# A decode kernel's result in two halves instead of four quarters, one store on each queue, and the last wait as an instruction of its own

## The chip, the cores and the metric

The kernel runs on one core of one Trainium2 chip. The metric is the device time of one execution in microseconds (us); a run is one execution. The profile's "span" is shorter: it goes from the first to the last of the program's own instructions. All timed runs quoted are of the state "fast", or "unknown" where a kernel was looked at once.

Names: PE is TensorE (matmuls), PEld its weight loads, DVE is VectorE, ACT is ScalarE, POOL is GpSimd, SP is SyncE (it issues the loads). A q after a name is that engine's instruction sequencer, and L687 is line 687 of the kernel.

## The reference, cut to what matters

One token for each of 4 batch entries attends over a cache of 8192 positions (16 query heads on 8 KV heads of 256). The output projection's result `s` is multiplied by a gate `g`, which comes from a small MLP, and added to the input.

```python
B, Sq, D = 4, 1, 448
Hq, Hkv, Sk, Dh = 16, 8, 8192, 256
...
x = A_x
xn = _layernorm(x, axis=-1)
s = _A_ref(xn, A_k_cache, A_v_cache, A_wq, A_wo)     # attention, then @ wo (4096 x 448)
g = _silu(_B_ref(xn, B_w1, B_w2, B_w3, B_w4))
return x + s * g                                     # 4 x 1 x 448, bf16
```

The two caches are 268 MB. The result is 4 rows of 448 numbers.

## The kernel before

SyncE streams K, V and the weights in. Of `wo`, the last heads' pieces ("LATE") are loaded last of all. The result is made in four quarters of D: quarter `i` lies on 4 of the 32 partitions that begin at `32 * i`, so that its matmuls run in their own 32 columns of TensorE, beside those of the three others (in the trace, the first four of the projection start at 651.411, 651.415, 651.418 and 651.421 us and are 0.21 to 0.22 us long each).

```python
NQD = 4
DQ, PQ = D // NQD, P // NQD                  # 112 columns, 32 partitions
...
def store(eng, i):
    eng.dma_start(out2d[:, i * DQ:(i + 1) * DQ], out_b[i * PQ:i * PQ + Bn, :]
                  ).then_inc(S["dout"], 16)
...
# SyncE, after its last load                 # ScalarE, after its last exp
sp.wait_ge(S["v_out"], 1)                    act.wait_ge(S["v_out"], 1)
store(sp, 0)                                 store(act, 2)
store(sp, 1)                                 store(act, 3)
sp.wait_ge(S["dout"], 16 * NQD)
...
def take(eng, name, n=1):                    # a wait with an update: an instruction of its own
    eng.wait_ge(S[name], n).then_inc(S[name], -n)
...
def f_o(hs, stop=False):                     # TensorE, the projection (L687)
    for hq in hs:
        for dh in range(NHALF):
            for i in range(NQD):
                ins = pe.matmul(o_ps[i * PQ:(i + 1) * PQ, 0:DQ],
                                OT[:, hq // REP, hq % REP, dh, :],
                                wo_sb[:, hq, dh, i * DQ:(i + 1) * DQ], ...)
...
take(pe, "dwl0", 16)                         # TensorE, the very end
f_o(LATE[0])
take(pe, "v_ot")
f_o(range(HQ - REP, HQ))
for i in range(1, len(LATE)):
    take(pe, "dwl%d" % i, 16)
    ins = f_o(LATE[i], i == len(LATE) - 1)
ins.then_inc(S["p_o"], 1)
...
v.wait_ge(S["p_o"], 1)                       # VectorE (L526, L528)
c(v.tensor_tensor(res[:, :], o_ps[:, 0:DQ], sg4[:, :], ALU.mult))
c.sync()
v.tensor_tensor(out_b[:, :], res[:, :], x4[:, :], ALU.add).then_inc(S["v_out"], 1)
```

A plain `wait_ge` with nothing after it but the end of the program is put on the next instruction of that engine; for SyncE that is the branch to the barrier at the program's end (in the raw records below it starts 0.017 us after the last landing of a store).

## Time and profile before

| | value |
|---|---|
| device time, median of the first 3 runs | 658.67 us (658.19 to 659.90) |
| span of the profiled run | 656.0 us |
| device time minus span of that run | 2.18 us |
| last piece of `wo` landed (semaphore records) | 652.378 us |
| from there to the end of the span | 3.620 us |

The view of stretches gives, for each stretch of time, its length, each engine's busy time (with the number of instructions), the granted TensorE clock as a share of full speed, the share of the DMA engines that is busy, and the rate. For the kernel before:

```profile
core 0: us, PE busy (x) PEld busy (x) DVE busy (x) ACT busy (x) POOL busy (x), PEclk, DMA share, GB/s
31.00:620.00 589.00, 510.73 (x9331) 445.18 (x9328) 246.01 (x496) 239.21 (x341) 9.40 (x58) 0.89 1.00 431
620.00:652.40 32.40, 29.26 (x499) 22.81 (x499) 11.11 (x25) 8.35 (x15) 0.20 (x1) 0.94 0.94 397
652.40:656.00 3.60, 0.38 (x8) 0.17 (x8) 0.55 (x2) 0.00 (x0) 0.00 (x0) 0.50 0.01 1
```

For 589 us the share of the DMA engines that is busy is 1.00: the kernel is bound by its loads. Only the last line, 3.6 us in which nothing is loaded, belongs to the change. The timeline of that tail (start, length, engine, line, what; in brackets the idle time before it and who ended it), kernel before, weight loads left out:

```profile
start us, us, engine line op out<-in xcount [idle before <-releaser]
651.41 0.93 PE L687 MATMUL pst<-wo_sb,OT 128*32 128x112 bf16 x40 [0.45 <-PEq L244]
...
652.51 0.38 PE L687 MATMUL pst<-wo_sb,OT 128*32 128x112 bf16 x8 [0.17 <-PEq L244]
652.94 0.27 DVE L526 TENSOR_TENSOR res<-pst,sg 128x112 f32<-128x112 f32 x1 [1.65 <-PE pst L687]
653.25 0.27 DVE L528 TENSOR_TENSOR out_b<-res,x 128x112 bf16<-128x112 f32 x1
653.55 0.66 SPq L184 DMA_DIRECT2D out_dram<-out_b  x2
653.55 0.62 ACTq L184 DMA_DIRECT2D out_dram<-out_b  x2
```

TensorE has done 40 of its last 48 matmuls when the last `wo` lands at 652.378; it waits, and does the last eight. Then two VectorE operations in series, then two stores on each queue.

The timeline leaves out waits, branches and drains. SyncE's last instructions, from the raw records of the same trace (start in us, kind, length in ns); the last landing of a store is at 655.252:

```
653.548 DMA_DIRECT2D 347
653.936 DMA_DIRECT2D 274
655.269 COMPARE_BRANCH 33      <- the branch that carries the wait for the stores
655.713 DRAIN 77               <- 0.444 us later
655.935 EVENT_SEMAPHORE 17     <- the barrier
```

### The profile page before, as it was taken

What the parts mean: (1) busy time and instruction counts of PE and PEld (TensorE: products, weight loads), DVE (VectorE), ACT (ScalarE), POOL (GpSimd) and SP (SyncE); (2) the same over time, 40 slices, a digit from 0 to 9 for tenths busy, and PEclk for the clock granted to TensorE, in tenths of its full rate; (3) what the DMA queues carried; (4) which work ended last, traced back from release to release, by engine and by line L of the source; (5) the groups of instructions that cost most, each with busy time, mean ns of one, the idle gap of its engine ahead of it and who ended that gap; (6) DMA issues with size and microseconds to landing.
All of it is one profiled execution on the core that took longest, in us unless ns stands there. A gap on an engine that the chain in (4) does not pass through costs nothing. (4 is left out here: it accounts for less than half of the span.)

```text
span 656.0 us, 22934 instructions
## 1 busy us (share of the span) xinstructions
PE 554.9 (85%) x9969; PEld 475.1 (72%) x9969; DVE 276.4 (42%) x593; ACT 256.2 (39%) x364; POOL 13.4 (2%) x77
## 2 busy tenths in 40 slices
PE   1899997988888988888897888898888898888897
PEld 0487886876766887677787766787677688766774
DVE  7453554443443443344443443444344443343441
ACT  4144544442433443334443333444333344433340
POOL 2000000000000000000000000000000000000000
PEclk9698999887899888789987888988778987888998
DMA  8999999999999999999999999999999999999996
GB/s 361 442 412 424 439 424 440 424 440 424 440 424 440 424 440 426 438 426 440 424 435 430 434 430 434 430 434 432 432 432 432 432 432 432 434 430 434 432 423 279
DMA packets 12369, 279.13 MB, mean 426 GB/s; under 512 B 1220, under 2 KB 3272, under 8 KB 3784
## 3 DMA queue, kind: packets, MB, share of 16 engines
q1 hardware_dynamic: 12336, 278.99, 99.3%
q8 instruction: 7, 0.11, 0.1%
q14 instruction: 2, 0.02, 0.0%
q10 hardware_dynamic: 24, 0.01, 0.0%
HBM read 278.99 MB, written 0.00 MB: 425 GB/s over the span
## 5 line engine op out<-in xcount | busy, mean ns | idle before, releaser
L588 PE MATMUL pst<-ident_b,kn 128*128 128x128 bf16 x4096 | 347.2, 239 | 79.0 <-PEq L244 76.4
L294 ACT ACTIVATE kT<-pst 128x1024 bf16<-128x1024 bf16 x224 | 229.5, 1025 | 360.7 <-ACTq L244 359.9
L588 PEld LDWEIGHTS pst<-ident_b,kn 128*128 128x128 bf16 x4096 | 275.4, 108 | 84.9 <-issue 84.3
L292 DVE COPY kT<-pst 128x1024 bf16<-128x1024 bf16 x288 | 197.5, 692 | 264.6 <-DVEq L244 264.6
L600 PE MATMUL psc<-qc,kT 128*128 128x2 bf16 x4096 | 178.4, 164 | 0.0
L600 PEld LDWEIGHTS psc<-qc,kT 128*128 128x128 bf16 x4096 | 157.4, 98 | 28.5 <-issue 28.1
L639 PE MATMUL psv<-vb,pT 128*4 128x512 bf16 x1056 | 86.3, 378 | 0.0
L618 PE MATMUL psm<-sel,po 128*128 128x2 f32 x272 | 36.8, 257 | 0.5 <-PEq L244 0.5
L618 PEld LDWEIGHTS psm<-sel,po 128*128 128x128 f32 x272 | 34.7, 196 | 0.9 <-issue 0.9
L639 PEld LDWEIGHTS psv<-vb,pT 128*4 128x4 bf16 x1056 | 22.2, 82 | 15.0 <-issue 0.5
L452 DVE TENSOR_REDUCE rmax<-psc 128x2 f32<-128x128 f32 x32 | 9.3, 292 | 48.5 <-DVEq L244 48.5
L470 DVE COPY po<-psv 128x512 f32<-128x512 f32 x34 | 23.5, 692 | 3.0 <-DVEq L244 2.3
L457 DVE TENSOR_REDUCE gmax<-psm 2x1 f32<-2x128 f32 x32 | 8.9, 279 | 34.7 <-DVEq L244 34.7
L316 ACT ACTIVATE pT<-psc,negb 128x64 bf16<-128x64 f32 x66 | 20.6, 333 | 5.4 <-ACTq L244 5.4
L612 PEld LDWEIGHTS psm<-diag,ones_f 2*128 2x128 f32 x66 | 14.1, 264 | 6.5 <-issue 5.7
L279 POOL COPY qc<-qT 128x4 bf16<-128x4 bf16 x32 | 5.9, 186 | 585.7 <-DVEq L469 568.4
L612 PE MATMUL psm<-diag,ones_f 2*128 2x2 f32 x66 | 16.8, 322 | 1.1 <-PEq L244 0.9
L316 ACT ACTIVATION_READ_ACCUMULATOR pT<-psc,negb 128x1 f32 x66 | 13.6, 206 | 0.0
L608 PEld LDWEIGHTS psm<-ident_f,rmax 128*2 128x2 f32 x32 | 2.6, 80 | 14.0 <-issue 14.0
L536 PE MATMUL pst<-ident_b,xn_b 4*128 4x4 bf16 x14 | 0.6, 161 | 13.6 <-DVE xn_b L365 8.9
L630 PE MATMUL psm<-rowsum,ones_f 128*128 128x2 f32 x64 | 11.6, 251 | 0.0
L536 PEld LDWEIGHTS pst<-ident_b,xn_b 4*128 4x128 bf16 x14 | 0.5, 99 | 13.6 <-issue 8.9
(101 smaller groups left out, 119.8 us busy)
## 6 DMA issues: line engine op xcount, KB each, us to landing
kn<-in_A_k_cache_dram SPq DMA_DIRECT2D x32, 4096.0 KB, 25.7
vb<-in_A_v_cache_dram SPq DMA_DIRECT2D x31, 4096.0 KB, 31.3
vb<-in_A_wq_dram SPq DMA_DIRECT2D x1, 3584.0 KB, 11.5
vb<-in_B_w_dram SPq DMA_DIRECT2D x2, 1568.0 KB, 16.4
wo_sb<-in_A_wo_dram SPq DMA_DIRECT2D x1, 2688.0 KB, 44.0
kn<-in_A_v_cache_dram SPq DMA_DIRECT2D x1, 2048.0 KB, 25.1
kn<-in_A_v_cache_dram SPq DMA_DIRECT2D x1, 1024.0 KB, 27.1
kn<-in_A_v_cache_dram SPq DMA_DIRECT2D x2, 512.0 KB, 28.3
```

The lines of the kernel that those rows point to most:

```text
L292: engine.tensor_copy(dst, src).then_inc(S["v_ev"], 1)
L294: engine.activation(dst, src, ACT.Copy).then_inc(S["a_ev"], 1)
L316: ins = act.activation(pv_p[:, :, hh], sc[:, :, hh], ACT.Exp, bias=negb[:, s, hh:hh + 1], scale=SCALE, accum_out=rowsum[:, s, hh:hh + 1])
L452: v.tensor_reduce(rmax[:, :], psc[h % 2][:, 0:NCH * REP].rearrange("p (k h) -> p h k", h=REP), AX.X, ALU.max).then_inc(S["v_rmax"], 1)
L457: v.tensor_reduce(gmax[:, :], psm[0:REP, 0:P], AX.X, ALU.max).then_inc(S["v_s"], 1)
L470: v.tensor_copy(po[:, slot], psv[:, 0:CP * DH]).then_inc(S["v_po"], 1)
L588: ins = pe.transpose(dst[:, t * P:(t + 1) * P], kn[:, h % 2, GC * j + kl, half * P:(half + 1) * P], ident_b[:, :])
L600: ins = pe.matmul(psc[h % 2][:, kk * REP:(kk + 1) * REP], kT[:, j % RING, t * P:(t + 1) * P], qc[:, h % 2, half, :], start=(half == 0), st ...
L612: pe.matmul(psm[:, P:P + REP], ones_f[0:REP, :], diag[:, :], start=True, stop=True).then_inc(S["p_m2"], 1)
L618: ins = pe.matmul(dst(dh)[:, 0:width], po[:, slot, i * DH + dh:(i + 1) * DH:NHALF], sel[:, i, 0:width], start=(i == 0), stop=(i == CP - 1))
L630: pe.matmul(psm[:, P + REP:P + 2 * REP], ones_f[:, :], rowsum[:, h % 2, :], start=True, stop=True)
L639: ins = pe.matmul(psv[o:o + CP * REP, 0:CP * DH], pT[:, h % 2, kk * REP:(kk + CP) * REP], src[:, kk:kk + CP, :].rearrange("p c d -> p (c d)"),
```

## The change

The intent: one store on each queue instead of two, which needs each store to cover half of D, hence halves instead of quarters; and no wait on the final branch. Cut to its core:

```diff
-    DQ, PQ = D // NQD, P // NQD
+    NDG = 2
+    DQ, PQ = D // NDG, P // NQD             # now 224 columns; still 32 partitions a group
+    DP = NDG * PQ                           # 64
...
-        res = sb("res", [P, DQ], F32)       # the same for x4, xn4, sg4, bout, out_b
+        res = sb("res", [DP, DQ], F32)
...
             store(sp, 0)
-            store(sp, 1)
-            sp.wait_ge(S["dout"], 16 * NQD)
+            take(sp, "dout", 16 * NDG)
...
-            store(act, 2)
-            store(act, 3)
+            store(act, 1)
...
-                for i in range(NQD):        # VectorE's prologue copies into x4 and xn4,
+                for i in range(NDG):        # TensorE's f_o and its two f32 products with selb
...
-            c(v.tensor_tensor(res[:, :], o_ps[:, 0:DQ], sg4[:, :], ALU.mult))
+            c(v.tensor_tensor(res[:, :], o_ps[0:DP, 0:DQ], sg4[:, :], ALU.mult))
```

More of the change, by code (lines that the diff above doesn't have):

```diff
@@ L61, in bass_recurrent_scan__gqa_block_cached__mixer_s_mlp__decode_kernel @@
     NQD = 4
-    DQ, PQ = D // NQD, P // NQD
-    assert D == NQD * DQ
+    NDG = 2
+    DQ, PQ = D // NDG, P // NQD
+    DP = NDG * PQ
+    assert D == NDG * DQ
     NCH = SK // P
@@ L138, in bass_recurrent_scan__gqa_block_cached__mixer_s_mlp__decode_kernel @@
         xn2_f = sb("xn2_f", [Bn, D], F32)
-        x4 = sb("x4", [P, DQ], F32)
-        xn4 = sb("xn4", [P, DQ], F32)
-        sg4 = sb("sg4", [P, DQ], F32)
-        res = sb("res", [P, DQ], F32)
+        x4 = sb("x4", [DP, DQ], F32)
+        xn4 = sb("xn4", [DP, DQ], F32)
+        sg4 = sb("sg4", [DP, DQ], F32)
+        res = sb("res", [DP, DQ], F32)
         xn2_b = sb("xn2_b", [Bn, DK, P // 2, 2], BF16)
         junk = sb("junk", [Bn, D], F32)
-        bout = sb("bout", [P, DQ], F32)
-        out_b = sb("out_b", [P, DQ], BF16)
+        bout = sb("bout", [DP, DQ], F32)
+        out_b = sb("out_b", [DP, DQ], BF16)
         st = sb("st", [Bn, 16], F32)
@@ L174, in bass_recurrent_scan__gqa_block_cached__mixer_s_mlp__decode_kernel @@
         h2_ps = psv
-        hs_ps = psm[:, 2 * P:2 * P + DQ]
+        hs_ps = psm[0:DP, 2 * P:2 * P + DQ]
         o_ps = pst[0]
@@ L573, in prog_pe @@
             take(pe, "v_h2")
-            for i in range(NQD):
+            for i in range(NDG):
                 ins = pe.matmul(hs_ps[i * PQ:(i + 1) * PQ, :], selb[:, :],
@@ L685, in f_o @@
                     for dh in range(NHALF):
-                        for i in range(NQD):
+                        for i in range(NDG):
                             ins = pe.matmul(o_ps[i * PQ:(i + 1) * PQ, 0:DQ],
@@ L732, in finish @@
                 take(pe, "v_a")
-                for i in range(NQD):
+                for i in range(NDG):
                     pe.matmul(o_ps[i * PQ:(i + 1) * PQ, 0:DQ], selb[:, :],
```

## The prediction

The four terms came to -0.36 - 0.36 + 0.22 + 0.6 = +0.1 us, from 658.67 to 658.8 us. No term is cut from it, only reasons, where the cuts are marked: in point 1 a general statement of how stores report landings (the trace of the kernel before shows four landings for each store, 16 in all), in point 4 a rule of when the clock falls and how that shifts between executions, which no trace had shown. The trace had shown half clock from 651.70 us on; the +0.6 within its range is the author's estimate. The figures for 224 columns are estimates from that trace, where matmuls of 112 columns in one group start 0.049 us apart at full clock and 0.093 at half, and those of the gate's f32 product 0.19 at half clock; doubled, that is about what the points say. That the wider rows cost nothing visible, and that only the branch costs the 0.44 us, were assumptions. In point 3 the trace has 216 ns at 56 columns and not 222, which makes it 1.05 ns a column, and still about +0.12.

> **What bounds it now.** Loads. The table of stretches shows the DMA share at 1.00 and 431 GB/s from 31 to 620 us, while TensorE waits for tiles in every pass. The semaphore landings put the last piece of wo at 652.38 us of a 656.00 us span. The change touches no load. It can move only the last 3.6 us (and a little of the prologue).
>
> **The tail now, read from the trace records (us).** Last wo lands 652.38; last eight matmuls (32 rows x 112) 652.51 to 652.89, their semaphore 652.915; VectorE multiply 652.94, 0.274 long; add 653.25, 0.274 long; the two queues issue their first stores at 653.55, their second at 653.85 (ScalarE) and 653.94 (SyncE). Landings come in four groups of four, 0.18 apart: 654.64-654.71, 654.82-654.89, 655.00-655.07, 655.18-655.25. SyncE's wait sits on a branch (655.269); its next instruction starts only at 655.713, 0.44 later. End barrier to 656.00.
>
> **What the change does, on that chain.**
>
> 1. Stores, -0.36: one store per queue leaves only the first two groups, so the last landing comes about 1.345 after the issue instead of 1.704. [...] Rows of 448 B instead of 224 B should cost nothing visible.
> 2. Wait, -0.36: as an instruction of its own it needs no branch. On GpSimd a semaphore instruction before the block's end is followed by the drain after 0.08 (632.252 to 632.333), where SyncE's branch took 0.44.
> 3. VectorE, +0.22: both result operations go from 112 to 224 columns on half the partitions. Tensor-tensor took 222 ns at 56 columns and 275 ns at 112, so about 0.95 ns a column: about +0.11 each, estimated.
> 4. TensorE, +0.1 to +0.95, estimate +0.6: four column groups become two, with twice the columns. 48 matmuls become 24, but each group still gets 12, of 224 columns. Starts in one group are 0.049 apart at full clock at 112; so about 0.096 at 224, and 0.187 at half clock. The clock records show half clock from 651.70. Starting at 651.41, the twelve then end near 653.6 instead of 652.9: no longer hidden behind the last load, but bound by TensorE itself. [...] this trace's half-clock stretches are multiples of 3.41. [...] if the clock is full, only +0.1 remains; if half throughout, +0.95.
> 5. Off the path: the f32 matmul of the gate becomes about 0.37 longer at half clock near 24.6, delaying the first transposes at 30.8. SyncE issues the third K load at 42.5 while the queue is busy until the wo landing at 47.3, so absorbed. Half as many prologue copies on VectorE: also absorbed. The f32 matmul at 648.3 ends before the piece that lands at 648.85 is taken.
>
> **Sum.** -0.36 -0.36 +0.22 +0.6 = +0.1 us. From 658.67: 658.8 us, range 657.6 to 660.0, mostly the scatter of runs (658.19 to 659.9 before). Faster by over 2%: 1%; within 2%: 98%; slower: 1%.
>
> **What will show it.** 8 landings instead of 16 on the result's semaphore, last about 1.35 after the issue; SyncE's drain about 0.1 after its wait; VectorE operations of about 0.385; last matmul's semaphore 0.1 to 0.95 later after the last wo landing than 0.537; DMA share and last wo landing unchanged.
>
> **What would make it wrong.** Full clock in the tail in most runs (then about -0.4); landings of 448 B rows slower; a branch that stays; a load that starts later because of the prologue.

## The result, and the profile after

| | before | after |
|---|---|---|
| median device time | 658.58 us (658.19 to 660.07, 6 runs) | 658.34 us (657.41 to 659.91, 6 runs) |
| ratio after to before | | 0.9991, 95% interval 0.9974 to 1.0007 |
| device time minus span | 2.18 us (the profiled run) | 1.67 us (mean of 6 runs, 1.61 to 1.81) |

A ratio here is the mean time of one kernel's fast runs over that of the other's fast runs of the same rounds, so it is not quite the ratio of the medians. The two kernels are the same within the noise.

The same two views, kernel after:

```profile
core 0: us, PE busy (x) PEld busy (x) DVE busy (x) ACT busy (x) POOL busy (x), PEclk, DMA share, GB/s
31.00:620.00 589.00, 511.11 (x9332) 445.64 (x9331) 245.94 (x496) 238.91 (x341) 9.40 (x58) 0.89 1.00 431
620.00:652.40 32.40, 29.12 (x465) 22.70 (x467) 11.21 (x25) 8.34 (x15) 0.20 (x1) 0.94 0.94 397
652.40:656.00 3.60, 1.62 (x18) 1.15 (x14) 0.77 (x2) 0.00 (x0) 0.00 (x0) 0.50 0.01 1
```

```profile
start us, us, engine line op out<-in xcount [idle before <-releaser]
...
651.61 2.41 PE L687 MATMUL pst<-wo_sb,OT 128*32 128x224 bf16 x24 [0.50 <-PEq L245]
654.06 0.38 DVE L526 TENSOR_TENSOR res<-pst,sg 64x224 f32<-64x224 f32 x1 [2.61 <-PE pst L687]
654.47 0.38 DVE L528 TENSOR_TENSOR out_b<-res,x 64x224 bf16<-64x224 f32 x1
654.88 0.35 SPq L186 DMA_DIRECT2D out_dram<-out_b  x1
654.89 0.28 ACTq L186 DMA_DIRECT2D out_dram<-out_b  x1
```

The loads are untouched: 1.00 and 431 GB/s as before. In the tail, the 24 matmuls are one block of 2.41 us without a gap. TensorE no longer waits for the last `wo`, which landed at 652.587; it runs 1.4 us behind it. And SyncE's end, from the raw records (last landing 656.291):

```
654.883 DMA_DIRECT2D 352
656.308 EVENT_SEMAPHORE 17     <- the wait, an instruction of its own
656.388 DRAIN 7                <- 0.080 us later
656.833 EVENT_SEMAPHORE 17     <- the barrier, 0.445 us after the drain
```

The gap of 0.44 us before the drain is gone, but one of the same size stands behind it.

The tail can be cut at four semaphore events: last `wo` landed, projection done, result ready, last store landed. All in us, from the traces:

| piece of the tail | before | after | difference |
|---|---|---|---|
| last `wo` landed to projection done (TensorE) | 0.537 | 1.445 | +0.908 |
| to result ready (VectorE) | 0.616 | 0.834 | +0.218 |
| to last landing of a store | 1.721 | 1.425 | -0.296 |
| to the end of the span (the barrier) | 0.746 | 0.559 | -0.187 |
| sum | 3.620 | 4.263 | +0.643 |

In these two traces the tail is 0.64 us longer after, the last `wo` lands 0.21 us later (652.587 against 652.378; the first load of weights is already 0.21 us later, 12.425 against 12.211), and the span is 0.85 us longer. Yet the device times of these two runs differ by only 0.35 us (658.53 against 658.18), because 0.5 us was saved outside the span. It lies after it: the traces go on to record semaphore updates after the last instruction, and the last of these comes 2.307 us after the end of the span before and 1.717 us after it in the kernel after. That saving was in nobody's forecast.

### The profile page after: what moved, and what is told of

Read it like the earlier page. It is cut to its first block, busy times and chain, and to the rows that moved or that the text cites. A ratio compares the mean times of both kernels' runs of the same rounds, so it can differ in the third digit from the quotient of the medians.

```text
span 656.9 us, 22864 instructions
## 1 busy us (share of the span) xinstructions
PE 556.3 (85%) x9937; PEld 476.3 (73%) x9937; DVE 276.5 (42%) x589; ACT 256.0 (39%) x364; POOL 13.4 (2%) x77
```

## The experiments

What was to be told apart: what makes TensorE late (the half clock, or two column groups as such); what the stall of 0.44 us hangs on (the branch with the wait, or something else); what the number of stores is worth; and where the 0.5 us after the span comes from. One idea could not be tried: quarters with one store on each queue.

All kernels below gave correct results. This table holds what their profiles show. The clock is the record over the last projection; "late" means that TensorE came late to its first matmul there, seen from the last landing of `wo`; that earlier work at half clock held it up is an estimate, from the fact that these three alone have a stretch of 6.83 us at half clock near 620 to 627 us. The last two columns look past the span. "Landing to 207" is the time from the last landing of a store to the first of a long row of updates that every trace has after its span (they begin with semaphore 207): it tells when the engines got on. "Late gap" is the time between the fifth and the sixth of the last nine updates of semaphore 2, which are the last updates of each trace.

| kernel | clock | TensorE | VectorE | stores | barrier | device minus span | landing to 207 | late gap |
|---|---|---|---|---|---|---|---|---|
| before | half | 0.537 | 0.616 | 1.721 | 0.746 | 2.18 | 1.404 | 0.502 |
| after | half | 1.445 | 0.834 | 1.425 | 0.559 | 1.68 | 0.976 | 0.099 |
| e1_wait_only | full, late | 0.533 | 0.617 | 1.727 | 0.801 | 2.20 | 1.459 | 0.503 |
| e2_branch_wait | full | 0.518 | 0.834 | 1.423 | 0.603 | 1.86 | 1.037 | 0.098 |
| e3_halves_four_stores | full, late | 0.892 | 0.833 | 1.716 | 0.801 | 1.78 | 1.459 | 0.099 |
| e5_halves_warm | full | 0.947 | 0.834 | 1.422 | 0.559 | 1.71 | 0.976 | 0.098 |
| p1_before_nop1 | half | 0.537 | 0.621 | 1.720 | 0.391 | 2.19 | 1.050 | 0.502 |
| p2_after_nop2 | full | 0.517 | 0.833 | 1.421 | 0.336 | 2.13 | 0.995 | 0.098 |
| p3_after_pe32 | full | 0.518 | 0.834 | 1.425 | 0.558 | 1.70 | 0.976 | 0.098 |
| p4_after_dve4 | half | 1.390 | 0.832 | 1.427 | 0.559 | 1.98 | 0.977 | 0.502 |
| k1_before_dve_less4 | full | 0.441 | 0.619 | 1.722 | 0.746 | 1.81 | 1.405 | 0.100 |
| k2_before_dve_less4_nop1 | full, late | 0.805 | 0.618 | 1.715 | 0.391 | 1.78 | 1.049 | 0.097 |

### Only the wait

```diff
-            sp.wait_ge(S["dout"], 16 * NQD)         # kernel before
+            take(sp, "dout", 16 * NQD)
```

> The kernel before with its last wait as an instruction of its own; four stores and quarters stay. My theory (the wait's form alone moves the end): last landing to the end of the span 0.56 us instead of 0.746, device time minus span about 1.65 us instead of 2.2, so about 0.7 us faster in device time; TensorE's, VectorE's and the stores' terms as before (0.54, 0.62 and 1.72 us). Rival (the 0.44 us stall depends on where in the instruction stream the instructions lie; here the stream is one longer than in both kernels): the stall is then elsewhere or gone, and the end is neither 0.746 nor 0.56 us.

Measured: 658.19 us (5 runs) against 658.53 us of the kernel before (9 runs), ratio 0.9995, interval 0.9981 to 1.0009: the same. The barrier took 0.801 us, not 0.56, and device time minus span stayed at 2.21 us (mean of 5). SyncE, raw records:

```
655.209 EVENT_SEMAPHORE 17
655.661 DRAIN 124              <- 0.452 us after the wait, although no wait is on a branch
655.931 EVENT_SEMAPHORE 17
```

My theory of the branch falls. With four stores the stall stands before the drain, whatever the form of the wait.

### Halves, with the wait on the branch

```diff
-            take(sp, "dout", 16 * NDG)              # kernel after
+            sp.wait_ge(S["dout"], 16 * NDG)
```

> The kernel after with its last wait back on the branch; two stores and halves stay. My theory: last landing to the end of the span back to 0.746 us, device time minus span back to about 2.2 us, so about 0.7 us slower than the kernel after and 0.4 to 0.6 us slower than the kernel before (TensorE +0.91, VectorE +0.22, stores -0.30). Rival (position in the stream, which is one shorter here): another value.

Measured: 657.82 us (5 runs) against 658.53 (9 runs), ratio 0.9991, interval 0.9977 to 1.0004. The expectation was wrong in both numbers, barrier and device time minus span (mean of 5: 1.70 us), and so in device time, 0.71 us under the kernel before instead of 0.4 to 0.6 us over it:

```
655.370 COMPARE_BRANCH 33
655.511 DRAIN 7                <- 0.141 us after the branch with the wait
655.939 EVENT_SEMAPHORE 17     <- the stall, 0.428 us, is behind the drain
```

So the form of the wait decides nothing: the branch with the wait on it shows no stall here. The four traces so far, and that of the halves with four stores below, share one rule instead. Count SyncE's recorded instructions from its first store: before has store, store, branch, then the stall, then the drain. After has store, wait, drain, then the stall, then the barrier. Here it is store, branch, drain, stall, barrier; in the kernel with only the wait, store, store, wait, stall, drain. The stall always stands between the third and the fourth. It belongs to a place in the instruction stream, and dropping a store moved the drain in front of it. Counted from the program's start, it is the place between the 79th and the 80th of SyncE's records in every trace of this document in which the stall can be seen (nine).

The place matters more than the barrier's time within the span says. Where the stall stands before the drain, the other engines wait for SyncE too; where it stands behind, they go on without it. From the last landing to the updates after the span it is 1.404 and 1.459 us in the first case (before; only the wait), 0.976 and 1.037 in the second (after; this kernel).

This run also answers the question of TensorE, because its TensorE program is the same as in the kernel after, while its clock in the tail happened to be full. Timeline of the kernel with halves and the wait on the branch:

```profile
start us, us, engine line op out<-in xcount [idle before <-releaser]
651.61 1.47 PE L687 MATMUL pst<-wo_sb,OT 128*32 128x224 bf16 x24 [0.53 <-PEq L245]
653.12 0.38 DVE L526 TENSOR_TENSOR res<-pst,sg 64x224 f32<-64x224 f32 x1 [1.71 <-PE pst L687]
```

Its view of stretches shows the clock of the tail, 1.00 where the kernel after had 0.50:

```profile
652.40:655.95 3.55, 0.68 (x12) 0.23 (x6) 0.77 (x2) 0.00 (x0) 0.00 (x0) 1.00 0.01 1
```

The same 24 matmuls from the same start (651.61) take 1.47 us instead of 2.41. The view of one line gives the length of one matmul (min/median/max, ns); first the kernel after, then this one:

```profile
L687 PE MATMUL pst<-wo_sb,OT x24: 319/391/392, 651.6 to 653.6; 128*32 128x224 bf16 x24
```

```profile
L687 PE MATMUL pst<-wo_sb,OT x24: 256/259/269, 651.6 to 652.8; 128*32 128x224 bf16 x24
```

In the raw starts, matmuls of one column group follow each other at 186.7 ns in the kernel after and at 95.5 ns here.

### Halves, with four stores

The wait is doubled to match; that line is left out here.

```diff
-            eng.dma_start(out2d[:, i * DQ:(i + 1) * DQ], out_b[i * PQ:i * PQ + Bn, :]
-                          ).then_inc(S["dout"], 16)
+            for c in range(2):
+                w = DQ // 2
+                eng.dma_start(out2d[:, i * DQ + c * w:i * DQ + (c + 1) * w],
+                              out_b[i * PQ:i * PQ + Bn, c * w:(c + 1) * w]
+                              ).then_inc(S["dout"], 16)
```

> The kernel after with each half stored by two stores of 112 columns. If the number of stores sets the last landing, it comes 1.72 us after the result is ready, as in the kernel before, instead of 1.425, in four groups about 0.18 us apart. If rows of 448 B were what made the two landings of the kernel after slower than forecast, the first two groups come as in the kernel before: 1.11 to 1.18 and 1.29 to 1.36 us.

Measured (one look): last landing 1.716 us after the result is ready. The first group came at 1.11 to 1.18 us and the second at 1.29 to 1.36, as in the kernel before; with rows of 448 B they came at 1.13 to 1.24 and 1.31 to 1.43. The store records are 14 ns long for a row of 224 B in the kernel before, and 24 to 32 ns for one of 448 B after. So the number of stores is worth 0.29 us (1.716 against 1.425), and the wider rows cost some 0.07 us of what four landings fewer on each queue would give.

### Halves, with TensorE kept busy

```diff
+                f_warm(2)
                 f_direct(NPIECE - ND)
+                f_warm(1)
                 take(pe, "v_po")
 ...
                 f_direct(NPIECE - 1).then_inc(S["p_pv"], 1)
+                f_warm(3)
```

> The kernel after with six dummy matmuls in TensorE's waits between 648 and 651.5 us, to keep the clock at full in the tail. My theory (two column groups at half clock make TensorE late): if the clock record then says 1.0 through the tail, the last projection's semaphore comes 0.6 to 0.7 us after the last wo landing instead of 1.445. Rival (the lateness is that of the loads or of the column groups alone): still over 1.2 us at full clock. If the clock stays at half, nothing changes and the run tells nothing.

Measured: 657.93 us (4 runs) against 658.53 (9 runs), ratio 0.9993, interval 0.9978 to 1.0009. The clock was full, but the term was 0.947 us, between what the two theories said. The trace shows why: the first matmuls of the projection start at 651.500, 651.691 and 651.881, one after each of my dummies, so that the dummies themselves made it late. This run tells nothing of the cause, and it does not show either that the dummies kept the clock full: it was full without them, too, in the three kernels named last here. The cause was settled by kernels with an untouched TensorE tail, whose clock fell one way or the other: at half clock 1.445 (after) and 1.390 (the kernel with four more clears), at full clock 0.518, 0.517 and 0.518 (wait on the branch; two idle instructions; tiny matmuls in the prologue).

### Moving SyncE's stream by one, and by two

```diff
+            for _ in range(1):                      # 2 in the kernel after
+                sp.sem_inc(S["nop"], 1)
             sp.wait_ge(S["v_out"], 1)
             store(sp, 0)
```

> The kernel before with one semaphore instruction that nothing waits for on SyncE, ahead of its first store, in idle time. The five traces agree on this rule: SyncE stalls 0.43 to 0.45 us once between the third and the fourth instruction counted from its first store (a silent branch not counted), whatever the wait's form. If so, one more instruction ahead moves the stall to behind the second store, where SyncE waits for landings anyway: last landing to the end of the span 0.30 us instead of 0.746, and no gap of 0.44 us between the wait and the drain. My first theory (the branch with the wait on it costs the 0.44 us) and any theory by which the stall follows the last landing: still 0.746 us.

> The kernel after with two such instructions on SyncE ahead of its store. Position rule: the stall moves from behind the drain to behind the store, and the last landing to the end of the span is about 0.28 us instead of 0.559. If the stall belongs to the drain and the barrier, it stays 0.559.

Measured: the barrier fell from 0.746 to 0.391 us with one instruction more in the kernel before, and from 0.559 to 0.336 us with two more in the kernel after. SyncE in the kernel before with one more (last landing 655.993):

```
656.010 COMPARE_BRANCH 33
656.169 DRAIN 7                <- 0.159 us after the branch; 0.444 without the extra instruction
656.321 EVENT_SEMAPHORE 17
```

The rule of position holds in both, and it foretold them; the gain is 0.09 and 0.06 us less than it said, since the branch still takes its 0.16 us and the longer stream of the kernel after 0.11 us from wait to drain. That the stall is still there, behind a store, cannot be seen in SyncE's records: it would lie in the time in which SyncE waits for the landings anyway. In device time the two were 658.25 us (6 runs, two of them at 659.77 and 661.18) against 658.18 (11 runs), ratio 1.0009, interval 0.9993 to 1.0025, and 657.75 us (4 runs), ratio 0.9993, interval 0.9979 to 1.0008: too small to see through the scatter of runs. In the kernel after with two more, device time minus span also rose, from 1.67 to 2.03 us (means of 6 and 4 runs), so that what was saved within the span was given back after it. The traces show most of the reason: in the kernel after, the stall behind the drain delays SyncE's own last instruction alone, which is the end of the span, and not the other engines. From the last landing to the updates after the span it was 0.976 us without the two instructions and 0.995 us with them: there was nothing left to save. In the kernel before, where the stall stood before the drain, the one instruction did save: 1.404 to 1.050 us.

### Whose stream sets the time after the span

```diff
+            for i in range(32):                     # TensorE, prologue of the kernel after
+                pe.matmul(psv[0:PVW, 0:8], pT[:, 0, 0:PVW], wq_sb[:, 0, 0:8], start=True, stop=True)
```
```diff
+            for i in range(4):                      # VectorE, prologue of the kernel after
+                v.memset(junk[:, i:i + 1], 0.0)
```

> The kernel after with 32 tiny matmuls (8 columns) on TensorE in the prologue, so that TensorE's stream is as long as in the kernel before (64 instructions, loads of weights with them). The device time minus the span is 2.13 to 2.25 us in every run of the quarter kernels and 1.61 to 1.85 us in every run of the half kernels. If the length of TensorE's stream sets it, it is 2.1 to 2.25 here; if VectorE's (four instructions), 1.6 to 1.85.

> The kernel after with four tiny clears on VectorE in the prologue, so that VectorE's stream is as long as in the kernel before. If VectorE's stream sets the device time minus the span, it is 2.1 to 2.25 us; if TensorE's, 1.6 to 1.85.

Measured (one look each): with TensorE's stream restored, device time minus span stayed at 1.70 us; with VectorE's restored it was 1.98 us, outside both forecasts. So not TensorE, and VectorE at least in part. The late gap of the table fits: 0.098 us in the first, 0.502 us in the second, as in the kernel before. VectorE's stream is thus worth 0.40 us here, too. The rest of the distance to 2.18 is largely a matter of where SyncE's stall stands (above), which ends the span later in the half kernels (from the end of the span to the updates after it: 0.66 us in the kernel before, 0.42 here).

The run with tiny matmuls had a surprise: 668.71 us, some 10 us longer (one look, state unknown). The view of stretches, that kernel first, then the kernel before:

```profile
40.00:45.00 5.00, 5.00 (x58) 5.00 (x56) 1.05 (x2) 1.33 (x2) 0.00 (x0) 0.50 1.05 378
45.00:50.00 5.00, 5.00 (x90) 4.75 (x87) 2.41 (x6) 2.05 (x2) 0.00 (x0) 0.65 0.12 42
```

```profile
40.00:45.00 5.00, 5.00 (x110) 3.58 (x111) 2.44 (x5) 1.71 (x2) 0.00 (x0) 1.00 1.09 395
45.00:50.00 5.00, 3.95 (x72) 3.17 (x63) 2.45 (x6) 1.60 (x2) 0.19 (x1) 1.00 1.07 445
```

The clock fell to half (its record says from 38.3 to 48.5 us), TensorE freed the first K tile later, the third K load was issued at 49.6 us instead of 42.5, and the DMA engines ran dry. The tiny matmuls themselves took 0.94 us, far less than this delay. So in this run the prologue was not off the critical path: TensorE did not free its first tile in time. Whether the matmuls of 8 columns are what brought the clock down was not tried.

### VectorE's stream shortened in the kernel before, alone and with SyncE's shifted

```diff
-            for t in (x4, xn4):                     # VectorE
-                c(v.memset(t[:, :], 0.0))
             c.sync()
 ...
-            v.sem_inc(S["dv0"], 16)
-            v.sem_inc(S["dv1"], 16)
+            for t in (x4, xn4):                     # GpSimd, at the end of its clears
+                c(gp.memset(t[:, :], 0.0))
 ...
+            gp.sem_inc(S["dv0"], 16)                # GpSimd, after its wait for v_qT
+            gp.sem_inc(S["dv1"], 16)
```

The second kernel also has the one idle instruction on SyncE.

> The kernel before with four of VectorE's prologue instructions (two clears, two semaphore increments) moved to GpSimd, so that VectorE's stream is as short as in the kernel after; SyncE, ScalarE and TensorE as before. If VectorE's stream length sets the device time minus the span (it was 1.7 with TensorE's stream restored, 2.0 with VectorE's restored), it is 1.6 to 1.85 us here instead of 2.13 to 2.25; if not, 2.13 to 2.25. The tail within the span as before: last landing to the end 0.746 us.

> Both: the kernel before with VectorE's stream shorter by four and one idle semaphore instruction on SyncE. Last landing to the end of the span about 0.39 us as with that instruction alone. If the two gains add, device time is 0.35 + 0.4 = about 0.75 us under the kernel before; if what SyncE saves within the span is given back after it, as in the kernel after with two such instructions, only 0.3 to 0.4 us.

Measured: device time minus span was 1.83 us (mean of 4 runs, 1.79 to 1.85) in the first and 1.79 us (5 runs) in the second, against 2.18 to 2.25 in the nine runs of the kernel before beside them. VectorE's stream is confirmed as a cause: four instructions moved to GpSimd save 0.38 us (mean 2.21 to 1.83) after the last of the program's own instructions. Moving them also made GpSimd's stream longer by four, but the late gap rules that out as the cause. It is 0.50 us in the four traces with 1324 records on VectorE (before, e1, p1, p4) and 0.10 us in the eight with 1320, whether GpSimd has 118 records or 122, SyncE 80 to 82, and TensorE its longer or its shorter stream. Two stalls are thus told apart, and they add up. From the last landing to the last update in the trace it is 3.05 us with both (before), 2.68 us without VectorE's (k1), 2.70 us without SyncE's (p1) and 2.30 us without either (k2). The first kernel took 657.89 us against 658.53, ratio 0.9992, interval 0.9976 to 1.0007. The second took 657.71 us against 658.53 (0.82 us less; 0.75 was expected), ratio 0.9988, interval 0.9975 to 1.0002, which still includes 1; its five runs, 657.45 to 658.00, all lie below the fastest of the nine of the kernel before, 658.18. It keeps quarters, four stores and the wait on the branch. Against the kernel after it was not run in the same rounds, so that it beats that one too is not shown.

The first of the two also gives quarters at full clock with TensorE not held up: 0.441 us from the last `wo` to the projection's end.

## Why the prediction was right or wrong, point by point

The forecast of the time held: 658.8 us (657.6 to 660.0) was said, 658.34 us measured, no difference that shows. Most of that is luck. The range was mostly the scatter of runs, so that almost any small sum would have fallen into it. And in the traced pair the errors cancelled: TensorE lost 0.3 us more than the estimate of 0.6, the stores gained 0.06 less, the barrier 0.17 less within the span, and against these stood 0.53 us after the span that nobody had counted.

1. Stores, forecast -0.36: right in mechanism (two groups of landings instead of four), mis-sized. It measured -0.296; the term "rows of 448 B instead of 224 B should cost nothing visible" was wrong by some 0.07 us, as the run with four narrow stores shows.
2. Wait, forecast -0.36: the step that failed. "As an instruction of its own it needs no branch" is not why the end came sooner. The wait's form alone gave +0.055 us with four stores (0.801 against 0.746) and -0.044 us with two (0.559 against 0.603). The stall sits at a place in SyncE's stream, and one store fewer put the drain ahead of it. Within the span that gained 0.14 us with the wait still on the branch (0.746 to 0.603) and 0.19 us in all; up to the updates after the span it gained 0.37 us with the wait on the branch (1.404 to 1.037) and 0.43 us in all (1.404 to 0.976). So the size of the forecast was near by luck. Comparing with GpSimd, whose stream is at another place, was no test of that.
3. VectorE, forecast +0.22: right, +0.218 (0.383 and 0.382 us for the two operations instead of 0.274).
4. TensorE, forecast +0.1 to +0.95 with the clock as the reason: right. At half clock it measured +0.908 (1.445 against 0.537), at full clock +0.077 (0.518 against 0.441). Four column groups had hidden most of the half clock behind the last load (0.537 us at half in the kernel before, 0.441 at full in k1); two do not (1.445 at half in the kernel after, 0.518 at full in e2). The starts of matmuls of 224 columns in one group show the same: 186.7 ns apart at half clock, 95.5 at full, where the forecast said 0.187 and 0.096 us.
5. Off the path: right for this change. The gate's f32 matmul got 0.36 us longer (0.60 to 0.96), the third K load was issued at 42.7 us instead of 42.5, and the DMA share stayed at 1.00. The run with tiny matmuls shows that this slack ends (third K load at 49.6 us, DMA share 0.12 from 45 to 50 us).
6. What the forecast lacked: the time after the span. It fell from 2.2 to 1.67 us, and VectorE's four prologue copies fewer, which I had written off as "also absorbed", are most of it: 0.38 us with four other instructions fewer in the kernel before (2.21 to 1.83), and 0.40 us by the late gap (0.502 to 0.099). The rest comes with the stall of point 2, which in the kernel after ends the span late while the other engines have gone on (SyncE's last instruction starts at 656.833 us, those of the others by 656.552).

Worked out from these terms, the change is worth 0.908 + 0.218 - 0.296 - 0.187 - 0.53 = +0.11 us where the tail runs at half clock, and 0.077 instead of 0.908, so -0.72 us, where it runs at full. The runs measured a median difference of -0.24 us, between the two. Which clock the untraced runs had is not known, so that this explains the median is an estimate and not shown.

Left open: why SyncE's stall stands where it does, and why VectorE's stream moves the end of the device time. That the engines' transfers of instructions are behind either is not shown. What the traces show are packets of 8192 B of the kind "instruction" around the end of the span (the first 0.31 us after it in the kernel before, 0.62 us in the kernel after). They move with SyncE's stream: in the three kernels with idle instructions ahead of the store, the first such packet near the end starts before SyncE's wait is over (655.982 against 656.010 us in p1, 655.270 against 655.279 in p2, 655.473 against 655.493 in k2), in the nine others 0.29 to 0.90 us after the span. This would fit a stall that moved and did not vanish; but in none of the nine does such a packet run during the stall, and no run separated these transfers from other causes.

## What to carry to other kernels

Here the tail that waits for its last load hid most of the slow compute (0.537 us at half clock in the kernel before, 0.441 at full in k1); with half the parallel column groups it did not (1.445 in the kernel after, 0.518 in e2). Before you halve them in such a tail, work out its length at half clock, too: of the twelve traces here, the clock was half there in four and full in eight. When a gap of some tenths of a microsecond stands after an instruction, do not take that instruction for its cause: move it by one place with an idle instruction and see whether the gap moves along (0.444 us behind the branch became 0.159 here). And read device time minus span, and the semaphore updates after the span, as well. Here a shorter instruction stream on VectorE, which is busy for 42% of the span in the kernel before, saved 0.38 us after the last instruction of the profile, and SyncE's stall at the very end of the span of the kernel after delayed nobody else (0.976 us from the last landing to the updates after the span with it, 0.995 with two idle instructions ahead).
